# Building the S4 convolution kernel's power tables from scaled activations in blocks of 224 channels, in place of argument matmuls in blocks of 48

## The chip, the cores and the metric

The kernel runs on one core of a Trainium2 chip. The metric is the device time of one execution in microseconds (us): the median of 5 runs is 1173.82 us (1171.51 to 1175.57). The engines are TensorE (PE in the profile, its weight loads PEld), the vector engine (DVE), the scalar engine (ACT), GpSimd (POOL) and SyncE (SP), which issues DMAs.

## The reference

Two layers run on separate inputs, and their outputs are joined along the last axis. A is a linear attention with softmax feature maps (16 heads of 28, sequence 2048, width 448). B, which matters here, is a diagonal state-space convolution: for each of 448 channels d there are N = 256 complex modes n, and

```
dt    = exp(log_dt)[:, None]
logdA = dt * (A_re + 1j * A_im)                       # 448 x 256
dB    = dt * (B_re + 1j * B_im)
P     = exp(logdA[:, :, None] * l[None, None, :])     # l = 0 .. 2047 (as bf16)
K     = einsum("dn,dnl,dn->dl", Cc, P, dB).real       # the convolution kernel
y     = irfft(rfft(pad(u)) * rfft(pad(K)))[:L] + u * Dskip
```

## The kernel before, in words

The program has three stretches. `hedgehog_attention` computes A. `ssm_coefficients` and `ssm_build_K` build K. `ssm_fft_conv` makes the sine and cosine constants of the Fourier steps and does the convolution in several passes through DRAM. Each stretch needs the memory or the results of the one before it, so they follow each other with little overlap. The instructions are written in program order; the Tile framework orders them on each engine's queue and adds the semaphore waits. Each queue runs in order.

K is built by splitting l = 64 h + l' with h = 0..31 and l' = 0..64. With w = exp(dt(A_re + i A_im)), the 128 modes of one chunk on the partitions (`nch` = 0, 1), U[h] = C dB w^(64h) and W[l'] = w^l', K is the real part of the sum over modes of U[h] W[l']. That is one pair of matmuls for each channel and chunk: `kps` += UR^T WR and UI^T WI, each 128 modes deep, 32 columns of weights (h) and 65 moving columns (l'). Four channels, one from each quarter g of the 448, use the four 32-column groups of the array (`tile_position=(0, 32*g)`), so four such matmuls run side by side. UI carries the minus sign.

Before the change `ssm_coefficients` makes dt A twice: on 4 x 112 channel rows, split into two bf16 parts and written to DRAM as `coefd` (lines 457 to 484), and once more in the layout modes x channels (`A_nd`, `TH_nd`, `CBR_nd`, `CBIN_nd`), from 12 transposing DMAs (line 504). `ssm_build_K` then loops over 2 chunks and 10 super-blocks `sb` of 12 x 4 = 48 channels (the last has 16):

- U is built by doubling on the vector engine (lines 650 to 655): k = 1, 2, 4, 8, 16, six bf16 operations each, on k x 48 elements; the powers w^(64k) (`P`, lines 566 to 587) are copied to dense 48-wide tiles by GpSimd first (lines 637, 638).
- W is built through PSUM: `coefblk` is loaded from `coefd`, and TensorE multiplies it by the ramp `Rconst` (lines 665, 667) to give the arguments l' dt A of 18 channels at a time in `args`, which has one buffer. ACT takes Exp of one half and twice Sin of the other (lines 684, 685, 687; Exp and Sin need different activation tables), and the vector engine multiplies (lines 693, 695).
- `emit_kmm` (lines 604, 606) does the pairs of matmuls of the super-block before. The sums of the first chunk are copied to `Ts` by ACT (line 611), those of the second added by the vector engine (line 613).

At the end `Ts` goes to DRAM as `kd` (line 705), and the Fourier part starts; its first vector operation that is long is `n1f` (line 759).

Of the kernel before, what the change touches and what calls it, by code (L numbers as in the profile page):

```python
# [451 lines left out]
def ssm_coefficients(tc, B_A_re, B_A_im, B_B_re, B_B_im, B_C_re, B_C_im, B_log_dt, coefd, base_pool):  # L452
    nc = tc.nc
    with tc.tile_pool(name="coef_in", bufs=1) as inp_pool, \
         tc.tile_pool(name="coef_w", bufs=1, side="right") as w:
        for dc in range(4):
            d0 = 112 * dc
            rows = 112
            tiles = {}
            for nm, src in (("Are", B_A_re), ("Aim", B_A_im)):  # L460
                t = inp_pool.tile([112, SSM_N], BF16, name=f"ci_{nm}", tag=nm)
                nc.sync.dma_start(out=t[:, :], in_=src[d0:d0 + rows, :])
                tiles[nm] = t
            ldt = inp_pool.tile([112, 1], BF16, name="ci_ldt", tag="ldt")
            nc.sync.dma_start(out=ldt[:, :], in_=B_log_dt[d0:d0 + rows].unsqueeze(1))
            dt32 = w.tile([112, 1], F32, name="dt32", tag="dt32")
            nc.scalar.activation(dt32[:, :], ldt[:, :], ACT.Exp)
            dtb = w.tile([112, 1], BF16, name="dtb", tag="dtb")
            nc.vector.tensor_copy(dtb[:, :], dt32[:, :])
            dt = w.tile([112, 1], F32, name="dt", tag="dt")  # L470
            nc.vector.tensor_copy(dt[:, :], dtb[:, :])
            a = w.tile([112, SSM_N], F32, name="a", tag="a")
            nc.vector.tensor_scalar_mul(a[:, :], tiles["Are"][:, :], dt[:, :])
            th = w.tile([112, SSM_N], F32, name="th", tag="th")
            nc.vector.tensor_scalar_mul(th[:, :], tiles["Aim"][:, :], dt[:, :])
            for ti, src_t in enumerate((a, th)):
                b1 = w.tile([112, SSM_N], BF16, name="b1", tag="b1")
                nc.vector.tensor_copy(b1[:, :], src_t[:, :])
                dif = w.tile([112, SSM_N], F32, name="dcf", tag="dcf")
                nc.vector.tensor_tensor(out=dif[:, :], in0=src_t[:, :], in1=b1[:, :], op=ALU.subtract)  # L480
                b2 = w.tile([112, SSM_N], BF16, name="b2", tag="b2")
                nc.vector.tensor_copy(b2[:, :], dif[:, :])
# [41 lines left out]
def build_R(tc, pool):  # L524
    nc = tc.nc
    with tc.tile_pool(name="rtmp", bufs=1) as tp:
        pidx = tp.tile([4, 1], I32, name="pidx")
# [16 lines left out]
    return R


def ssm_build_K(tc, coefd, kd, A_nd, TH_nd, CBR_nd, CBIN_nd, base_pool, dbg=False):
# [4 lines left out]
    with tc.tile_pool(name="k_const", bufs=1) as cpool, \
         tc.tile_pool(name="k_ts", bufs=1) as tspool, \
         tc.tile_pool(name="k_coef", bufs=2) as coefpool, \
         tc.tile_pool(name="k_hi", bufs=2) as hipool, \
         tc.tile_pool(name="k_tab", bufs=2) as tabpool, \
         tc.tile_pool(name="k_psarg", bufs=1, space=bass.MemoryType.PSUM) as psa_pool, \
         tc.tile_pool(name="k_psk", bufs=1, space=bass.MemoryType.PSUM) as psk_pool:
# [4 lines left out]
        for nch in range(2):
            P = {}
            amp1 = base_pool.tile([128, D_MODEL], F32, name="amp1", tag="amp1")
            nc.scalar.activation(amp1[:, :], A_nd[:, nch, :], ACT.Exp, scale=64.0)
            c1 = base_pool.tile([128, D_MODEL], F32, name="c1", tag="c1")
            nc.scalar.activation(c1[:, :], TH_nd[:, nch, :], ACT.Sin, bias=bias_hp[:, :], scale=64.0)
            s1 = base_pool.tile([128, D_MODEL], F32, name="s1", tag="s1")
            nc.scalar.activation(s1[:, :], TH_nd[:, nch, :], ACT.Sin, scale=-64.0)  # L570
            pr = base_pool.tile([128, D_MODEL], BF16, name="p1r", tag="p1r")
            pim = base_pool.tile([128, D_MODEL], BF16, name="p1i", tag="p1i")
            nc.vector.tensor_tensor(out=pr[:, :], in0=amp1[:, :], in1=c1[:, :], op=ALU.mult)
            nc.vector.tensor_tensor(out=pim[:, :], in0=amp1[:, :], in1=s1[:, :], op=ALU.mult)
            P[1] = (pr, pim)
# [12 lines left out]
            pending = []  # L588

            def emit_kmm(item):  # L590
                sbp, nqp, URp, UIp, WRp, WIp, nchp = item
                half = (nqp + 1) // 2
                stripes = [(0, half)]
                if nqp > half:
                    stripes.append((half, nqp))
                for si_, (q0, q1) in enumerate(stripes):
                    nqs = q1 - q0
                    kps = psk_pool.tile([128, 512], F32, name="kps", tag=f"kps{si_}")
                    for dql in range(q0, q1):
                        cs = dql - q0  # L600
                        for g in range(4):
                            slot = 4 * dql + g
                            outap = kps[32 * g:32 * (g + 1), cs * N_LO:(cs + 1) * N_LO]
                            nc.tensor.matmul(outap, lhsT=URp[:, :, slot], rhs=WRp[:, slot, :],  # L604
                                             start=True, stop=False, tile_position=(0, 32 * g))
                            nc.tensor.matmul(outap, lhsT=UIp[:, :, slot], rhs=WIp[:, slot, :],  # L606
                                             start=False, stop=True, tile_position=(0, 32 * g))
                    dq0 = sbp + q0
                    in_view = kps[:, 0:nqs * N_LO].rearrange("p (c l) -> p l c", c=nqs)
                    if nchp == 0:  # L610
                        nc.scalar.copy(Ts[:, :, dq0:dq0 + nqs], in_view)
                    else:
                        nc.vector.tensor_tensor(out=Ts[:, :, dq0:dq0 + nqs],
                                                in0=Ts[:, :, dq0:dq0 + nqs], in1=in_view, op=ALU.add)
# [469 lines left out]
```

## Time and profile before

| | us |
|---|---|
| median of 5 runs | 1173.82 |
| the profiled execution | 1177.62 |
| its span, first to last instruction | 1175.8 |
| busy in it: DVE, PE, ACT, POOL | 591.9, 539.4, 463.6, 101.6 |
| attention, start to 308.3 | 308.3 |
| coefficients and transposes, to 362.7 | 54.4 |
| the loop that builds K, to 773.5 | 410.8 |
| `kd` write and Fourier part, to the end | 402.3 |

The profile is of one execution. No engine is busy for more than half of the span, so shares over the whole span say little here; the stages have to be read one at a time.

### The profile page before, as it was taken

The numbers are of one execution on the slowest core, as the hardware profiler recorded it, in microseconds if no ns is written. First come the engines' busy times: TensorE is split into PE (matmuls) and PEld (weight loads), VectorE is DVE, ScalarE is ACT, GpSimd is POOL, SyncE is SP. The second block draws the span as 40 slices with busy tenths as digits, with TensorE's granted clock in tenths as the row PEclk, the third lists the DMA queues.
The fourth block names the chain that finished last, engine by engine and source line by source line (L and its number), as shares of the span: only waits on it lengthen the run. The fifth ranks groups of instructions, "written<-read, shape, count | busy, mean of one in ns | idle before, by whom it ended". The sixth has DMA issues, their size and how long they took to land.

```text
span 1175.8 us, 13968 instructions
## 1 busy us (share of the span) xinstructions
PE 539.4 (46%) x5285; PEld 251.0 (21%) x5291; DVE 591.9 (50%) x1288; ACT 463.6 (39%) x488; POOL 101.6 (9%) x260
## 2 busy tenths in 40 slices
PE   1986543846802433334334444402433444263298
PEld 0221100511201333333233333300111111010021
DVE  1339337526639765594756767429322224832500
ACT  0113320001216778878688788724212222031000
POOL 1000010000004221131211110010000000010000
PEclk9995655667965555555555555555555555555555
DMA  5000000000230000000000000050675666057511
GB/s 127 1 0 1 0 0 0 4 7 0 81 71 10 4 3 4 4 3 3 3 4 3 3 5 3 3 95 0 170 220 167 149 150 238 16 140 186 221 31 31
DMA packets 68011, 63.63 MB, mean 54 GB/s; under 512 B 33704, under 2 KB 64608, under 8 KB 67712
## 3 DMA queue, kind: packets, MB, share of 16 engines
q1 hardware_dynamic: 34554, 32.59, 10.3%
q10 hardware_dynamic: 31758, 23.73, 7.6%
q0 software_dynamic: 1632, 6.42, 1.6%
q8 instruction: 41, 0.67, 0.2%
q14 instruction: 26, 0.21, 0.1%
HBM read 30.73 MB, written 28.52 MB: 50 GB/s over the span
## 4 chain that ended last, share of the span: by engine, by line
DVE 33%; PE 29%; DMA 19%; ACT 9%; issue 7%; ACTq 1%; SPq 0%; POOL 0%; DVEq 0%; POOLq 0%
PE args L665 3%; DVE WR L693 3%; PE args L667 3%; PE ps_qk L195 3%; ACT L685 3%; PE ops L1013 2%; ACT CL L685 2%; PE ops L1011 2%; DVE UR L652 2%; DVE rt L650 2%; DVE rt L653 2%; DVE UI L655 2%; DMA xin<-kd 2%; PE num_ps L396 2%; DMA s2k<-SD_u 2%
## 5 line engine op out<-in xcount | busy, mean ns | idle before, releaser
L604 PE MATMUL kps<-WR,UR 128*32 128x65 bf16 x896 | 53.5, 257 | 203.3 <-DVE WR L693 198.2
L665 PE MATMUL args<-Rconst,coefblk 4*128 4x65 bf16 x896 | 105.1, 239 | 77.9 <-ACT SL L687 43.0
L665 PEld LDWEIGHTS <-coefblk 4*128 4x128 bf16 x896 | 96.7, 126 | 151.0 <-issue 145.4
L667 PEld LDWEIGHTS <-coefblk 4*128 4x128 bf16 x896 | 98.5, 128 | 42.5 <-issue 42.5
L667 PE MATMUL args<-Rconst,coefblk 4*128 4x65 bf16 x896 | 105.8, 240 | 0.0
L875 PE MATMUL psA<-xin,FA 32*128 32x448 bf16 x128 | 51.8, 565 | 97.7 <-DVE stgA L888 34.5
L684 ACT ACTIVATE E<-args 128x1170 bf16<-128x1170 f32 (+3 forms) x58 | 58.5, 1008 | 68.9 <-PE args L667 68.9
L693 DVE TENSOR_TENSOR WR<-E,CL 128x1170 bf16<-128x1170 bf16 (+3 forms) x58 | 39.6, 682 | 71.0 <-ACT CL L685 71.0
L685 ACT ACT_TABLE_LOAD x58 | 74.4, 1283 | 1.0
L684 ACT ACT_TABLE_LOAD x57 | 73.1, 1283 | 3.9 <-DVE WI L695 2.4
L888 DVE CAST stgA<-psA 128x1792 bf16<-128x1792 f32 x16 | 32.4, 2022 | 70.2 <-PE psA L875 43.2
L685 ACT ACTIVATE CL<-args,bias_hp 128x1170 bf16<-128x1170 f32 (+3 forms) x58 | 63.7, 1099 | 0.7
L412 ACT CAST rbc_sb<-rbc_ps 128x512 bf16<-128x512 f32 (+1 forms) x16 | 9.3, 585 | 133.7 <-PE rbc_ps L405 133.3
L687 ACT ACTIVATE SL<-args 128x1170 bf16<-128x1170 f32 (+3 forms) x58 | 58.0, 1000 | 0.0
L886 ACT CAST stgA<-psA 128x1792 bf16<-128x1792 f32 x16 | 26.4, 1652 | 79.1 <-PE psA L875 45.1
L604 PEld LDWEIGHTS <-UR 128*32 128x32 bf16 x896 | 37.0, 159 | 80.6 <-issue 62.3
L1011 PE MATMUL ops<-ZA,IA 128*32 128x448 bf16 x64 | 35.4, 556 | 34.5 <-DMA ZA<-ZD 34.5
L195 PE MATMUL ps_qk<-xT,Wqkv 128*128 128x512 bf16 (+3 forms) x125 | 37.3, 405 | 29.3 <-DMA xT<-in_A_x_dram 26.0
L909 PE MATMUL xps<-s2k,CB 128*32 128x448 bf16 x256 | 27.4, 534 | 47.2 <-DMA s2k<-SD_u 23.3
L606 PE MATMUL kps<-WI,UI 128*32 128x65 bf16 x896 | 43.9, 255 | 6.4 <-DVE WI L695 5.1
L875 PEld LDWEIGHTS <-FA 32*128 32x128 bf16 x128 | 17.0, 134 | 131.9 <-issue 103.9
L606 PEld LDWEIGHTS <-UI 128*32 128x32 bf16 x896 | 37.3, 163 | 31.1 <-issue 25.8
(265 smaller groups left out, 1152.2 us busy)
## 6 DMA issues: line engine op xcount, KB each, us to landing
ZA<-ZD SPq DMA_DIRECT2D x1, 7168.0 KB
SD_u<-stgA SPq DMA_DIRECT2D x8, 448.0 KB
SD_u<-stgA ACTq DMA_DIRECT2D x8, 448.0 KB
SD_k<-stgA SPq DMA_DIRECT2D x8, 448.0 KB
SD_k<-stgA ACTq DMA_DIRECT2D x8, 448.0 KB
s2k<-SD_u ACTq DMA_DIRECT2D x3, 896.0 KB
s2k<-SD_u SPq DMA_DIRECT2D x3, 896.0 KB
s2k<-SD_k ACTq DMA_DIRECT2D x3, 896.0 KB
```

Source lines behind the costliest of these rows:

```text
L195: nc.tensor.matmul(ps[plo:phi, sc * 512:(sc + 1) * 512], lhsT=Wt[dci][dplo:dphi, fcol0:fcol0 + frows], rhs=xT[dci][dplo:dphi, sc * 512:(sc ...
L604: nc.tensor.matmul(outap, lhsT=URp[:, :, slot], rhs=WRp[:, slot, :], start=True, stop=False, tile_position=(0, 32 * g))
L606: nc.tensor.matmul(outap, lhsT=UIp[:, :, slot], rhs=WIp[:, slot, :], start=False, stop=True, tile_position=(0, 32 * g))
L665: nc.tensor.matmul(args[:, j * 512 + si * N_LO:j * 512 + (si + 1) * N_LO], lhsT=coef[0:4, slot, :], rhs=R[0:4, 0, :], start=True, stop=True)
L667: nc.tensor.matmul(args[:, j * 512 + (3 + si) * N_LO:j * 512 + (4 + si) * N_LO], lhsT=coef[0:4, slot, :], rhs=R[0:4, 1, :], start=True, st ...
L684: nc.scalar.activation(E[:, b0:b0 + nb, 0:ns * N_LO], argview(0), ACT.Exp)
L685: nc.scalar.activation(CL[:, b0:b0 + nb, 0:ns * N_LO], argview(3 * N_LO), ACT.Sin, bias=bias_hp[:, :])
L687: nc.scalar.activation(SL[:, b0:b0 + nb, 0:ns * N_LO], argview(3 * N_LO), ACT.Sin)
L693: nc.vector.tensor_tensor(out=wr_v, in0=E[:, b0:b0 + nb, 0:ns * N_LO], in1=CL[:, b0:b0 + nb, 0:ns * N_LO], op=ALU.mult)
L875: nc.tensor.matmul(ps[:, n2l * 512:n2l * 512 + D_MODEL], lhsT=FA2[0:32, :], rhs=xt[0:32, 4 * j + n2l, :], start=True, stop=True,)
L888: nc.vector.tensor_copy(stg[:, jr:jr + 4, :], in_view)
L1011: nc.tensor.matmul(ops[32 * g2:32 * (g2 + 1), 0:D_MODEL], lhsT=IA[:, :], rhs=ZA[:, m2, :], start=True, stop=False, tile_position=(0, 32 * g2))
```

## The change

`coefd`, `build_R` and everything that read them go: the 4 x 112 rows of coefficients, their DMAs, `coefblk`, the argument matmuls, the GpSimd copies. W is computed straight from `A_nd` and `TH_nd`: for each l' one ACT instruction with `scale=l'` on 224 channels. The channel block grows from 48 to 224 (`h` = 0, 1; 56 from each quarter), so that there are four blocks in all (2 chunks x 2 halves), B0 to B3 below. Only l' = 0..48 come from ACT; l' = 49..64 are w^32 W[l'-32], one complex product on the vector engine (`_cmul`), and w^32 is `Q32`. `E` holds all 48 exponentials of a block, the sines come in 8 chunks of 6 l' in two buffers each. W is now laid out with l' outside and channels inside, so a matmul's moving operand `WR[:, :, slot]` has a step of 224 elements (448 bytes) where it was contiguous, and the weights `UR[:, :, slot]` have a step of 224 elements where it was 48. `WR` and `WI` have one buffer for all blocks, `UR` and `UI` two, `kps` two.

```diff
-def ssm_coefficients(tc, ..., B_log_dt, coefd, base_pool):
+def ssm_coefficients(tc, ..., B_log_dt, base_pool):
-        for dc in range(4):
...
-                nc.sync.dma_start(out=coefd[2 * ti, d0:d0 + rows, :], in_=b1[:, :])
-                nc.scalar.dma_start(out=coefd[2 * ti + 1, d0:d0 + rows, :], in_=b2[:, :])
...
+def _cmul(nc, out_r, out_i, ar, ai, brb, bib, t1, t2, sub):
+    nc.vector.tensor_tensor(out=t1, in0=ar, in1=brb, op=ALU.mult)
+    nc.vector.tensor_tensor(out=t2, in0=ai, in1=bib, op=ALU.mult)
+    nc.vector.tensor_tensor(out=out_r, in0=t1, in1=t2, op=ALU.subtract)
+    nc.vector.tensor_tensor(out=t1, in0=ar, in1=bib, op=ALU.mult)
+    nc.vector.tensor_tensor(out=t2, in0=ai, in1=brb, op=ALU.mult)
+    nc.vector.tensor_tensor(out=out_i, in0=t1, in1=t2, op=ALU.add)
...
-            for sb in range(0, NDQ, SBQ):
+            for h in range(2):
+                q_off = HQ * h
+                def dv(t2d):
+                    return t2d.rearrange("p (g q) -> p g q", g=4)[:, :, q_off:q_off + HQ]
...
                 for k in (1, 2, 4, 8, 16):
                     pr, pim = P[k]
-                    nc.gpsimd.tensor_copy(cr[:, 0:nds]..., dview(pr[:, :]))
-                    nc.gpsimd.tensor_copy(ci_[:, 0:nds]..., dview(pim[:, :]))
+                    prb = dv(pr[:, :]).unsqueeze(1).to_broadcast([128, k, 4, HQ])
+                    pib = dv(pim[:, :]).unsqueeze(1).to_broadcast([128, k, 4, HQ])
+                    _cmul(nc, gq(UR[:, k:2 * k, :]), gq(UI[:, k:2 * k, :]), gq(UR[:, 0:k, :]), gq(UI[:, 0:k, :]),
+                          prb, pib, gq(t1[:, 0:k, :]), gq(t2[:, 0:k, :]), False)
...
-                        nc.tensor.matmul(args[...], lhsT=coef[0:4, slot, :], rhs=R[0:4, 0, :], start=True, stop=True)
-                        nc.tensor.matmul(args[...], lhsT=coef[0:4, slot, :], rhs=R[0:4, 1, :], start=True, stop=True)
...
-                        nc.scalar.activation(E[:, b0:b0 + nb, 0:ns * N_LO], argview(0), ACT.Exp)
+                for l in range(1, LA):
+                    nc.scalar.activation(E[:, l - 1, :]..., dv(A_nd[:, nch, :]), ACT.Exp, scale=float(l))
+                for l0 in range(1, LA, CH):
+                    C = tabpool.tile([128, CH, NS], BF16, name="CL", tag="CL")
+                    S = tabpool.tile([128, CH, NS], BF16, name="SL", tag="SL")
+                    for l in range(l0, l0 + CH):
+                        nc.scalar.activation(C[:, l - l0, :]..., dv(TH_nd[:, nch, :]), ACT.Sin, bias=bias_hp[:, :], scale=float(l))
+                        nc.scalar.activation(S[:, l - l0, :]..., dv(TH_nd[:, nch, :]), ACT.Sin, scale=float(l))
+                    nc.vector.tensor_tensor(out=WR[:, l0:l0 + CH, :], in0=E[:, l0 - 1:l0 - 1 + CH, :], in1=C[:, :, :], op=ALU.mult)
+                    nc.vector.tensor_tensor(out=WI[:, l0:l0 + CH, :], in0=E[:, l0 - 1:l0 - 1 + CH, :], in1=S[:, :, :], op=ALU.mult)
+                nt = N_LO - LA
+                _cmul(nc, gq(WR[:, LA:N_LO, :]), gq(WI[:, LA:N_LO, :]), gq(WR[:, LA - 32:N_LO - 32, :]),
+                      gq(WI[:, LA - 32:N_LO - 32, :]), qrb, qib, gq(t1[:, 0:nt, :]), gq(t2[:, 0:nt, :]), False)
...
-                            nc.tensor.matmul(outap, lhsT=URp[:, :, slot], rhs=WRp[:, slot, :],
+                            nc.tensor.matmul(outap, lhsT=UR[:, :, slot], rhs=WR[:, :, slot],
                                              start=True, stop=False, tile_position=(0, 32 * g))
```

How the queues stand now is shown at three places. The first is ACT's queue in the loop. Before, each group of up to 18 channels has two table loads, an Exp that waits for TensorE, and two Sin:

```order
L684 ACT_TABLE_LOAD [waits DVE_49]
L684 ACTIVATE E<-args 128x1170 [waits PE_49]
L685 ACT_TABLE_LOAD
L685 ACTIVATE CL<-args,bias_hp 128x1170 [waits Activation_49]
L687 ACTIVATE SL<-args 128x1170 [waits Activation_49]
```

Now, at the passage from block B0 to B1 (line 572 is Exp, 578 and 580 are Sin, 604 is the copy of `kps`, with the line numbers of the changed kernel):

```order
L580 ACTIVATE SL<-TH_nd 128x224
L572 ACT_TABLE_LOAD
L572 ACTIVATE E<-A_nd 128x224 [waits DVE_49]
L572 ACTIVATE E<-A_nd 128x224 x22
L604 CAST Ts<-kps 128x65x7 [waits PE_49]
L572 ACTIVATE E<-A_nd 128x224 x4
L604 CAST Ts<-kps 128x65x7 [waits PE_49]
```

The 48 Exp of B1 stand together behind one table load, with the eight copies of B0's sums between them; the sines of B1 follow behind all of these.

The second place is the vector engine's queue where a block begins. Before, the first steps of the doubling are on 48 elements and the products wait for ACT alone:

```order
L650 TENSOR_TENSOR rt_4534<-UR,pc8r 128x384 [waits DVE_49]
L651 TENSOR_TENSOR rt_4535<-UI,pc8i 128x384
L652 TENSOR_TENSOR UR<-rt_4534,rt_4535 128x384 [waits DVE_49]
L693 TENSOR_TENSOR WR<-E,CL 128x1170 [waits Activation_49]
L653 TENSOR_TENSOR rt_4534<-UR,pc8i 128x384 [waits DVE_49]
```

Now, in B1 (494 to 499 are `_cmul`, 582 and 584 the products):

```order
L498 TENSOR_TENSOR rt_2858<-UI,p8r 128x1792
L582 TENSOR_TENSOR WR<-E,CL 128x1344 [waits PE_49,Activation_49]
L499 TENSOR_TENSOR UI<-rt_2857,rt_2858 128x1792 [waits DVE_49]
L584 TENSOR_TENSOR WI<-E,SL 128x1344 [waits PE_49,Activation_49]
L494 TENSOR_TENSOR rt_2857<-UR,p16r 128x3584 [waits DVE_49]
L495 TENSOR_TENSOR rt_2858<-UI,p16i 128x3584
L582 TENSOR_TENSOR WR<-E,CL 128x1344 [waits Activation_49]
L496 TENSOR_TENSOR UR<-rt_2857,rt_2858 128x3584 [waits DVE_49]
```

The long steps of the doubling now stand between the products of the first chunks, and the first product of a block waits for TensorE too, since `WR` has one buffer.

The third place is the end of a block on the same queue, in B0:

```order
L494 TENSOR_TENSOR rt_2174<-WR,p1rl 128x3584 [waits DVE_49]
L495 TENSOR_TENSOR rt_2175<-WI,p1il 128x3584 [waits DVE_49]
L582 TENSOR_TENSOR WR<-E,CL 128x1344 [waits Activation_49]
L584 TENSOR_TENSOR WI<-E,SL 128x1344 [waits Activation_49]
L496 TENSOR_TENSOR WR<-rt_2174,rt_2175 128x3584 [waits DVE_49]
L582 TENSOR_TENSOR WR<-E,CL 128x1344 [waits Activation_49]
L584 TENSOR_TENSOR WI<-E,SL 128x1344 [waits Activation_49]
L497 TENSOR_TENSOR rt_2174<-WR,p1il 128x3584 [waits DVE_49]
L498 TENSOR_TENSOR rt_2175<-WI,p1rl 128x3584
L499 TENSOR_TENSOR WI<-rt_2174,rt_2175 128x3584 [waits DVE_49]
```

The product for l' = 49..64 is begun after chunk 5, and its last three operations stand behind the products of chunk 7; the matmuls of the block wait for the last of them.

## Rows read from the trace of the kernel before

**Rows 1.** Busy time by stage (windows view; after each sum, the instruction count).

```profile
core 0: us, PE busy (x) PEld busy (x) DVE busy (x) ACT busy (x) POOL busy (x), PEclk, DMA share, GB/s
0.00:308.30 308.30, 190.84 (x1006) 59.58 (x1012) 140.91 (x221) 50.08 (x63) 8.40 (x27) 0.73 0.06 14
308.30:362.70 54.40, 15.26 (x89) 6.67 (x89) 31.75 (x91) 10.39 (x19) 2.06 (x6) 0.69 0.32 83
362.70:773.50 410.80, 157.46 (x3548) 140.08 (x3547) 268.61 (x811) 330.17 (x311) 73.44 (x197) 0.50 0.02 4
773.50:1175.80 402.30, 175.79 (x643) 44.69 (x643) 150.63 (x168) 72.96 (x97) 17.67 (x30) 0.51 0.47 132
```

**Rows 2.** Waits in the loop, longest first (us in total, times, longest).

```profile
PE kps L604 <- DVE WR L693: 198.2, 54, 9.6
DVE WR L693 <- ACT CL L685: 71.0, 27, 5.4
ACT E L684 <- PE args L667: 68.9, 53, 5.5
```

**Rows 3.** Chain that ended last (start us, us, what): around the loop.

```profile
328.85 1.22 ACTq L504
...
354.53 2.47 DMA tin_Cre<-in_B_C_re_dram
...
360.21 0.68 ACT c L568
...
773.54 15.27 DMA kd<-Ts
...
789.49 4.10 DVE n1f L759
```

**Rows 4.** ACT, 305 to 790 us, by form (count, busy us, mean ns, idle before).

```profile
L685 ACT ACT_TABLE_LOAD x58 | 74.4, 1283 | 1.0
L684 ACT ACT_TABLE_LOAD x57 | 73.1, 1283 | 3.9 <-DVE WI L695 2.4 <-DVE UI L655 0.5
...
L684 ACT ACTIVATE E<-args 128x1170 bf16<-128x1170 f32 x36 | 41.3, 1146 | 52.2 <-PE args L667 52.2
...
L684 ACT ACTIVATE E<-args 128x780 bf16<-128x780 f32 x18 | 14.8, 821 | 15.6 <-PE args L667 15.6
...
L611 ACT CAST Ts<-kps 128x390 bf16<-128x390 f32 x18 | 9.2, 511 | 1.9 <-PE kps L606 1.9
...
L568 ACT ACTIVATE c<-TH_nd,bias_hp 128x448 f32<-128x448 f32 x2 | 1.3, 668 | 3.3 <-DVE bias_hp L561 3.3
...
L566 ACT ACTIVATE amp<-A_nd 128x448 f32<-128x448 f32 x2 | 1.2, 576 | 10.4 <-DVE ttmp L516 10.4
```

**Rows 5.** Timeline: two activations of ACT back to back (start us, us).

```profile
486.42 1.24 ACT L685 ACTIVATE CL<-args,bias_hp 128x1170 bf16<-128x1170 f32 x1
487.56 1.14 ACT L687 ACTIVATE SL<-args 128x1170 bf16<-128x1170 f32 x1
```

**Rows 6.** DVE, 305 to 790 us, by form.

```profile
L613 DVE TENSOR_TENSOR Ts<-Ts,kps 128x390 bf16<-128x390 bf16 x18 | 10.0, 558 | 15.0 <-PE kps L606 15.0
...
L650 DVE TENSOR_TENSOR rt<-UR,pc16r 128x768 bf16<-128x768 bf16 x18 | 10.0, 557 | 1.5
...
L650 DVE TENSOR_TENSOR rt<-UR,pc8r 128x384 bf16<-128x384 bf16 x18 | 6.4, 358 | 1.4
...
L573 DVE TENSOR_TENSOR p1r<-amp,c 128x448 bf16<-128x448 f32 x2 | 1.2, 620 | 0.7 <-ACT c L568 0.7
```

**Rows 7.** Timeline of PE inside `emit_kmm` (start us, us; x4: four merged).

```profile
484.14 0.32 PE L604 MATMUL kps<-WR,UR 128*32 128x65 bf16 x4
...
484.20 0.32 PE L606 MATMUL kps<-WI,UI 128*32 128x65 bf16 x4
...
484.27 0.32 PE L604 MATMUL kps<-WR,UR 128*32 128x65 bf16 x4
```

**Rows 8.** Weight loads: 128 contiguous columns, and 32 columns with a step.

```profile
L665 PEld LDWEIGHTS <-coefblk 4*128 4x128 bf16 x896 | 96.7, 126 | 151.0 <-issue 145.4 <-DMA coefblk<-coefd 3.2 <-PE args L667 0.4
...
L604 PEld LDWEIGHTS <-UR 128*32 128x32 bf16 x896 | 37.0, 159 | 80.6 <-issue 62.3 <-DVE WR L693 9.9 <-DVE UR L652 7.4
```

More of the change, by code (lines that the diff above doesn't have):

```diff
@@ L449, with ssm_coefficients @@
 N_ARG = 2 * N_LO
-def ssm_coefficients(tc, B_A_re, B_A_im, B_B_re, B_B_im, B_C_re, B_C_im, B_log_dt, coefd, base_pool):
+def ssm_coefficients(tc, B_A_re, B_A_im, B_B_re, B_B_im, B_C_re, B_C_im, B_log_dt, base_pool):
     nc = tc.nc
-    with tc.tile_pool(name="coef_in", bufs=1) as inp_pool, \
-         tc.tile_pool(name="coef_w", bufs=1, side="right") as w:
-        for dc in range(4):
[L457 to L482, printed above, removed]
-                nc.sync.dma_start(out=coefd[2 * ti, d0:d0 + rows, :], in_=b1[:, :])
-                nc.scalar.dma_start(out=coefd[2 * ti + 1, d0:d0 + rows, :], in_=b2[:, :])
     A_nd = base_pool.tile([128, 2, D_MODEL], F32, name="A_nd")
@@ L562, in ssm_build_K, with make_pow @@
         Ts = tspool.tile([128, N_LO, NDQ], BF16, name="Ts")
+        WR = wpool.tile([128, N_LO, NS], BF16, name="WR")
+        WI = wpool.tile([128, N_LO, NS], BF16, name="WI")
+        nc.gpsimd.memset(WR[:, 0, :], 1.0)
+        nc.gpsimd.memset(WI[:, 0, :], 0.0)
         for nch in range(2):
[L564 to L575, printed above, removed]
+            def make_pow(scale, tagp, neg_sin):
+                amp = base_pool.tile([128, D_MODEL], F32, name="amp", tag="amp")
+                nc.scalar.activation(amp[:, :], A_nd[:, nch, :], ACT.Exp, scale=float(scale))
+                cv = base_pool.tile([128, D_MODEL], F32, name="cv", tag="cv")
+                nc.scalar.activation(cv[:, :], TH_nd[:, nch, :], ACT.Sin, bias=bias_hp[:, :], scale=float(scale))
+                sv = base_pool.tile([128, D_MODEL], F32, name="sv", tag="sv")
+                nc.scalar.activation(sv[:, :], TH_nd[:, nch, :], ACT.Sin,
+                                     scale=float(-scale if neg_sin else scale))
+                pr = base_pool.tile([128, D_MODEL], BF16, name=f"p1r{tagp}", tag=f"p1r{tagp}")
+                pi = base_pool.tile([128, D_MODEL], BF16, name=f"p1i{tagp}", tag=f"p1i{tagp}")
+                nc.vector.tensor_tensor(out=pr[:, :], in0=amp[:, :], in1=cv[:, :], op=ALU.mult)
+                nc.vector.tensor_tensor(out=pi[:, :], in0=amp[:, :], in1=sv[:, :], op=ALU.mult)
+                return pr, pi
+            P = {1: make_pow(64.0, "h", True)}
+            Q32 = make_pow(32.0, "l", False)
             for k in (2, 4, 8, 16):
@@ L587, in ssm_build_K @@
                 P[k] = (nr, ni)
[L588 to L603, printed above, removed]
-                            nc.tensor.matmul(outap, lhsT=URp[:, :, slot], rhs=WRp[:, slot, :],
[L605 to L614, printed above, removed]
@@ new lines, in ssm_build_K @@
+                nt = N_LO - LA
+                qrb = dv(Q32[0][:, :]).unsqueeze(1).to_broadcast([128, nt, 4, HQ])
+                qib = dv(Q32[1][:, :]).unsqueeze(1).to_broadcast([128, nt, 4, HQ])
+                _cmul(nc, gq(WR[:, LA:N_LO, :]), gq(WI[:, LA:N_LO, :]), gq(WR[:, LA - 32:N_LO - 32, :]),
+                      gq(WI[:, LA - 32:N_LO - 32, :]), qrb, qib, gq(t1[:, 0:nt, :]), gq(t2[:, 0:nt, :]), False)
+                for q0 in range(0, HQ, 7):
+                    kps = psk_pool.tile([128, 512], F32, name="kps", tag="kps")
+                    for cs in range(7):
+                        for g in range(4):
+                            slot = HQ * g + q0 + cs
+                            outap = kps[32 * g:32 * (g + 1), cs * N_LO:(cs + 1) * N_LO]
+                            nc.tensor.matmul(outap, lhsT=UR[:, :, slot], rhs=WR[:, :, slot],
+                                             start=True, stop=False, tile_position=(0, 32 * g))
+                            nc.tensor.matmul(outap, lhsT=UI[:, :, slot], rhs=WI[:, :, slot],
+                                             start=False, stop=True, tile_position=(0, 32 * g))
+                    dq0 = q_off + q0
+                    in_view = kps[:, 0:7 * N_LO].rearrange("p (c l) -> p l c", c=7)
+                    if nch == 0:
+                        nc.scalar.copy(Ts[:, :, dq0:dq0 + 7], in_view)
+                    else:
+                        nc.vector.tensor_tensor(out=Ts[:, :, dq0:dq0 + 7],
+                                                in0=Ts[:, :, dq0:dq0 + 7], in1=in_view, op=ALU.add)
```

144 lines of the change are left out of this document (29 added, 115 removed).

## The prediction

> **What bounds the kernel now.** I read the busy time by stage first [rows 1]. The loop that builds K takes 410.8 us, and the stages before and after it (308.3 + 54.4, and 402.3) hold almost nothing that the change touches. In the loop ACT is busy 330.2 us, DVE 268.6, PE 157.5. Then the waits [rows 2]: PE stands 198.2 us before its K matmuls for DVE's product, DVE 71.0 us for ACT's sine, ACT 68.9 us for PE's arguments. So it is a ring through one `args` buffer, in which ACT works longest. Then what ACT does [rows 4]: of its 330 us, 74.4 + 73.1 = 147.5 us are 115 table loads of 1283 ns, more than Exp or either Sin costs. Last, the chain of waits for the ends of the loop [rows 3]: the transposes run from 328.85 to 354.53 + 2.47 = 357.0, the first cosine starts at 360.21, `kd` is sent at 773.54, lands 15.27 later, and the Fourier part's vector work starts at 789.49.
>
> The profiled execution took 1177.62 us, 1.8 above its span; the median of the runs, 1173.82, is 3.8 below it. I sum against the profiled execution and take off the 3.8 at the end.
>
> **Prices.** DVE, bf16: 557 ns for 768 elements and 358 for 384 [rows 6], so 0.518 ns per element and 0.16 us fixed: 224 elements 0.275 us, 448 0.39, 896 0.62, 1344 0.86, 1792 1.09, 3584 2.02. With f32 operands, 448 elements cost 0.62. ACT: Exp on 1170 and 780 elements takes 1146 and 821 ns, 0.833 ns per element [rows 4]. From the 448-element forms that read SBUF (576 ns, with a bias tile 668) 224 elements less make 389 and 482 ns. A sine that follows another starts 0.10 us before its end (486.42 + 1.24 against 487.56) [rows 5]; so I charge 0.29 for Exp, 0.29 + 0.38 = 0.67 for a Cos/Sin pair, 4.0 for a chunk of 6, 13.9 for 48 Exp. If the 0.10 is not won between short ones, a chunk is 5.2 and the Exp 18.7. A copy of `kps` (455 elements) is 0.57 on ACT (511 for 390) and 0.63 on DVE (558 for 390). PE: four real matmuls start each 0.13 us, four imaginary ones between (484.14, 484.20, 484.27) [rows 7], so 8 in 0.13 us and 448 per block in 7.3 us.
>
> One price the trace lacks: a moving operand with a step. Below, it can cost nothing (7.3 us a block). Above, the nearest row is the weight load with a step, 159 ns for 32 columns against 126 for 128 contiguous ones [rows 8]: 5.0 ns a column, so 65 columns take 323 ns, a group's two matmuls 0.65, 56 rounds 36.4 us. I take twice the contiguous price, 14.6 us, nearer the low end, because the weights had a step already and four such loads hide within each 0.065 us of the pace above; I keep both ends. The Trainium skill ("Advanced Engine Details and Errata", section Memory Cachelines) says that SBUF is read in 16-byte lines and an access that changes line each time pays. It speaks against this layout, where each of the 65 columns is on its own line; it gives no figure, and by it the sum moves from the low end toward the upper one. No row here shows it for a moving operand.
>
> **Part by part.** *Removed.* The coefficient rows cost the path only where they delay the transposes behind the last output copies: I credit 3 us of the gap before 328.85 (bounds 0 and 8). The GpSimd copies (73 us busy) and the loads of `coefblk` lay beside other work: 0. The argument matmuls, and with them ACT's 68.9 us of waits, go. *Start.* The 12 transposes stay, so they end at 354.0. The bias tile still comes after them, the first cosine about 5.5 later. Then DVE stands between it and the first product of B0: 22 operations on 448 elements in f32 for the powers and w^32, at 0.62 or a little less, 12.9 us, and the doubling to k = 4 with two operations of k = 8, 9.6 (five at 0.275, six at 0.39, six at 0.62, two at 1.09): 22.5 us. First product: 382. ACT needs 19 us for the same stretch and waits.
>
> *A block* has on DVE: doubling 6 x (0.275 + 0.39 + 0.62 + 1.09 + 2.02) = 26.4, products 16 x 0.86 = 13.8, the l' >= 49 product 6 x 2.02 = 12.1, and 14 us of powers per mode chunk. On ACT: 13.9 + 8 x 4.0 and table loads. I walk the queues from each block's first product (t = 0).
>
> B0: DVE does 8 products, 4 steps of k = 8 and 6 of k = 16 interleaved: 6.9 + 4.4 + 12.1 = 23.4. ACT's chunk 5 needs the buffer freed there: done 27.4, chunk 6 at 32.0, chunk 7 at 36.6 (with the next chunk's cosine and sine). Last product 38.6, last three operations of the tail 44.7. ACT then does load 1.3, Exp 13.9, eight copies 4.6, load 1.3, chunk 4.0: 63.7. DVE from 44.7: doubling to k = 4, 7.7, ten operations of powers 6.6, five of k = 8 5.5: 64.5. PE's 7.3 or 14.6 us lie beside this. B0 takes 64.5.
>
> B1: products of chunks 0 to 2 with the long steps, 5.2 + 1.1 + 12.1 = 18.4; chunk 4 done 22.4; then the next chunk's amplitude with two loads, 3.2, chunk 5 at 29.4, 6 at 34.6, 7 at 38.6; last product 40.6, tail 47.3. ACT to the next chunk 0: 40.6 + 25.1 = 65.7; DVE 47.3 + 18 = 65.3. B1 takes 65.8.
>
> B2: no amplitude, so last product 37.4, tail 43.5. ACT 37.4 + 1.3 + 13.9 + 1.3 + 4.0 = 57.9; DVE 43.5 + 7.7 + 2.2 + eight adds 5.0 = 58.4. B2 takes 58.4.
>
> B3: as B0 to 44.7, then the matmuls 7.3 and the last add: 52.7.
>
> Sum 241.4; PE at 14.6 adds 1.7 (copies later on ACT), 3.0, 0 and 7.3, so 12. `kd` is sent at 382 + 241.4 + 12 = 635.5 in place of 773.5: 138 us earlier. What follows has its instructions and waits unchanged: 402.3. 1177.6 - 138 = 1039.6, less 3.8: **1036 us**.
>
> Bounds: PE at 7.3 and 5 us less at the start give 1019. Without the 0.10 us overlap the four blocks grow by 8.5, 10.6, 9 and 2.1 by the same walk: 1066. The Trainium skill ("VectorE: DVE Perf Modes", section on the TRN2 errata) says that VectorE and ScalarE pay a fixed latency for each instruction with an SBUF source and advises tiles of 512 or more; 576 instructions on 224 elements go against it. The row agrees that about 0.2 of the 0.39 us is fixed, and the rule's time is this 1066.
>
> **The rivals.**
> 1. *The strided matmuls decide.* At the upper price, 36.4 us a block, ACT's copies and then `WR`'s single buffer hold the next block: B0 passes at 44.7 + 36.4 + 6.9 = 88.0 in place of 64.5, B1 at 90.6 in place of 65.8, B2 at 79.9 in place of 58.4, B3 29.1 later: 99 us over the sum at 7.3 (1024): 1123. For it: [rows 8]. Against it: the pace of [rows 7] with stepped weights. 13%.
> 2. *DVE loses its rate.* The doubling and the tail now read a third operand in pieces of 56 out of 448, repeated. If this went at about 1.04 ns per element, the rate of the add that reads PSUM (558 ns for 390), 41,664 + 21,504 elements a block cost 33 us more, on the engine that is nearly always late: +120 of 132: 1156. Against it: today's repeated operand, in pieces of 48, runs at 0.518. 8%. This is also how the change could do little.
> 3. *Slower: the four column groups stop overlapping.* If their stepped reads wait for one another, the 448 matmuls of a block stand one behind another at up to 323 ns: 145 us a block. Above 15 us a block all four blocks pay; the sum is 1024 + 4k - 47 for k us a block, level with before at k = 49, 0.11 us per matmul, seven times today's 16 ns. At 323 ns it is 1557, at half that 1268. For it: the upper price is 20 times today's pace if nothing overlaps. Against it: stepped weight loads overlap now. 5%.
>
> **How the numbers follow.** The walk with its bounds (1019 to 1066) has 70%, rival 1 13%, rival 2 8%, rival 3 5%; 4% are left for a walk that is too slow on handovers nobody waits on, under 1010. The range 1010 to 1125 leaves out rivals 2 and 3, that edge and part of rival 1. A measurement tells 0.2% (2.3 us): faster 0.94, within 0.01, slower 0.05.
>
> **What the profile of the changed kernel would show.** ACT in the loop at about 17 table loads and 576 short activations of 0.39 and 0.48 us that start 0.29 and 0.38 apart. DVE busy some 250 us of a loop of about 255, doubling steps of 2.0 us at 3584 elements (3.9 would be rival 2). The K matmuls in four bursts of 7 to 15 us, with ACT's copies behind them; bursts of 36 us and a wait of DVE's first product for PE are rival 1, matmuls without overlap rival 3. GpSimd empty. `kd` near 636. The forecast is wrong if the gap between blocks is set by PE, or if the start of the loop moves by more than 8 us.

## The result, and the profile after

The changed kernel takes 1000.24 us (median of 8 runs, 998.98 to 1003.29) against 1174.27 (15 runs): ratio 0.852, 95% interval 0.850 to 0.853. That is 36 us less than forecast and 10 us below the low end of the range. The direction and the place of the gain were right, the size was not.

The profiled execution took 999.33 us (span 997.5). Busy time by stage, columns as in [rows 1]:

```profile
core 0: us, PE busy (x) PEld busy (x) DVE busy (x) ACT busy (x) POOL busy (x), PEclk, DMA share, GB/s
0.00:307.80 307.80, 190.62 (x1000) 58.91 (x1006) 139.69 (x219) 49.35 (x62) 8.39 (x27) 0.74 0.06 13
307.80:358.50 50.70, 14.89 (x59) 5.22 (x58) 19.38 (x38) 16.17 (x34) 0.51 (x2) 0.69 0.25 66
358.50:600.30 241.80, 53.95 (x1792) 52.49 (x1792) 227.63 (x278) 207.48 (x596) 0.13 (x1) 0.59 0.01 3
600.30:997.50 397.20, 174.11 (x643) 43.85 (x643) 150.39 (x168) 72.84 (x97) 17.61 (x30) 0.52 0.47 133
```

The loop takes 241.8 us in place of 410.8, and now DVE (227.6 us busy) and ACT (207.5) nearly fill it. The chain of waits shows the same marks as [rows 3]; the forecast had `kd` sent at 635.5:

```profile
351.00 2.29 DMA tin_Cre<-in_B_C_re_dram
...
600.33 15.02 DMA kd<-Ts
615.85 4.05 DVE n1f L664
```

From `kd` to the end it is 397.2 us, 5.1 less than before. So the profiled run is 40.3 us under the forecast's 1039.6 for a profiled execution: 35.2 of it up to `kd`, 5.1 behind it.

ACT from 358 to 601 us by form (answers to [rows 4]: count, busy us, mean ns, idle before):

```profile
L578 ACT ACTIVATE CL<-TH_nd,bias_hp 128x224 bf16<-128x224 f32 x192 | 86.7, 468 | 8.0 <-DVE WR L582 8.0
L580 ACT ACTIVATE SL<-TH_nd 128x224 bf16<-128x224 f32 x192 | 68.8, 374 | 2.5 <-DVE WI L584 2.3
L572 ACT ACTIVATE E<-A_nd 128x224 bf16<-128x224 f32 x174 | 50.8, 379 | 0.1
L604 ACT CAST Ts<-kps 128x455 bf16<-128x455 f32 x16 | 10.3, 642 | 0.8 <-PE kps L599 0.4
L572 ACT ACT_TABLE_LOAD x5 | 6.4, 1283 | 0.1
L578 ACT ACT_TABLE_LOAD x5 | 6.4, 1283 | 0.0
```

Forecast were 0.48, 0.39, 0.39 and 0.57 us: the prices from [rows 4] held but for the copies, which took 0.64 (1.1 us more for all 16), and 115 table loads became 14 in this stretch. DVE by form (370 to 620 us, answers to [rows 6]):

```profile
L582 DVE TENSOR_TENSOR WR<-E,CL 128x1344 bf16<-128x1344 bf16 x32 | 27.2, 850 | 2.4 <-ACT CL L578 2.4
L606 DVE TENSOR_TENSOR Ts<-Ts,kps 128x455 bf16<-128x455 bf16 x16 | 10.7, 667 | 9.2 <-PE kps L599 9.2
...
L494 DVE TENSOR_TENSOR rt<-UR,p16r 128x3584 bf16<-128x3584 bf16 x4 | 8.1, 2016 | 0.0
```

Forecast were 0.86, 0.63 and 2.02: again the prices held (the adds took 0.67), and rival 2 (3.9 us for the longest) is out. But a duration is not what an instruction costs its queue. DVE's timeline (start us, us) at the end of B0:

```profile
410.28 0.85 DVE L582 TENSOR_TENSOR WR<-E,CL 128x1344 bf16<-128x1344 bf16 x1
411.05 0.85 DVE L584 TENSOR_TENSOR WI<-E,SL 128x1344 bf16<-128x1344 bf16 x1
411.82 2.02 DVE L497 TENSOR_TENSOR rt<-WR,p1il 128x3584 bf16<-128x3584 bf16 x1
413.75 2.02 DVE L498 TENSOR_TENSOR rt<-WI,p1rl 128x3584 bf16<-128x3584 bf16 x1
415.80 2.03 DVE L499 TENSOR_TENSOR WI<-rt,rt 128x3584 bf16<-128x3584 bf16 x1
```

A product of 0.85 is followed after 0.77, an operation of 2.02 after 1.93: DVE starts the next 0.08 us before the end. One that needs the result just made waits it out (L499 reads what L498 wrote: 2.05), and so does one that writes over a tile just read (an L496 of 0.28 us from 418.36, and the L497 behind it, which refills its operand, starts at 418.67). The trace of the kernel before shows the same, a little ahead of the place of [rows 5] (DVE's timeline):

```profile
480.81 0.76 DVE L693 TENSOR_TENSOR WR<-E,CL 128x1170 bf16<-128x1170 bf16 x1
481.49 0.37 DVE L654 TENSOR_TENSOR rt<-UI,pc8r 128x384 bf16<-128x384 bf16 x1
```

Here 0.76 is followed after 0.68.

PE in the last block (timeline; answers to [rows 7]):

```profile
585.83 0.38 PE L597 MATMUL kps<-WR,UR 128*32 128x65 bf16 x4
585.96 0.36 PE L599 MATMUL kps<-WI,UI 128*32 128x65 bf16 x4
586.08 0.36 PE L597 MATMUL kps<-WR,UR 128*32 128x65 bf16 x4
...
586.30 0.37 PE L597 MATMUL kps<-WR,UR 128*32 128x65 bf16 x4
```

Eight matmuls take 0.23 us here, 0.13 before: 13 us a block.

### The profile page after: what moved, and what is told of

Its sections match the earlier page's. It is cut to its first block, busy times and chain, and to the rows that moved or that the text cites. A ratio compares the mean times of both kernels' runs of the same rounds, so it can differ in the third digit from the quotient of the medians.

```text
span 997.5 us, 9371 instructions
## 1 busy us (share of the span) xinstructions
PE 433.6 (43%) x3493; PEld 160.5 (16%) x3499; DVE 537.1 (54%) x701; ACT 345.9 (35%) x788; POOL 26.6 (3%) x60
## 4 chain that ended last, share of the span: by engine, by line
DVE 34%; PE 31%; DMA 22%; ACT 8%; issue 4%; ACTq 1%; SPq 0%; DVEq 0%; POOLq 0%
PE ps_qk L195 4%; PE ops L918 3%; PE ops L916 3%; PE kps L599 3%; PE kps L597 2%; DMA xin<-kd 2%; PE num_ps L396 2%; DMA s2k<-SD_u 2%; DVE WI L584 2%; DVE WR L582 2%; PE psA L780 2%; PE ps_pq L268 2%; DMA SD_u<-stgA 2%; DVE rt L498 2%; DVE rt L497 2%
## 5 line engine op out<-in xcount | busy, mean ns | idle before, releaser
L578 ACT ACTIVATE CL<-TH_nd,bias_hp 128x224 bf16<-128x224 f32 x192 | 86.7, 468 | 8.0 <-DVE WR L582 8.0
L597 PEld LDWEIGHTS <-UR 128*32 128x32 bf16 x896 | 46.6, 136 | 215.4 <-issue 154.0
L580 ACT ACTIVATE SL<-TH_nd 128x224 bf16<-128x224 f32 x192 | 68.8, 374 | 2.5 <-DVE WI L584 2.3
L572 ACT ACTIVATE E<-A_nd 128x224 bf16<-128x224 f32 x192 | 56.0, 378 | 0.1
L599 PEld LDWEIGHTS <-UI 128*32 128x32 bf16 x896 | 46.2, 135 | 6.5 <-DVE WI L499 6.5
L881 PE MATMUL zps<-YF,IB 32*128 32x448 bf16 x64 | 22.9, 530 | 41.8 <-DVE YF L868 24.4
L893 DVE CAST Zs<-zps 128x448 bf16<-128x448 f32 x32 | 20.0, 625 | 33.6 <-PE zps L884 32.1
L780 PEld LDWEIGHTS <-FA 32*128 32x128 bf16 x128 | 16.7, 133 | 131.5 <-issue 78.8
L891 ACT CAST Zs<-zps 128x448 bf16<-128x448 f32 x32 | 17.0, 532 | 60.0 <-PE zps L884 30.1
L918 PE MATMUL ops<-UD,IDT 32*32 32x448 bf16 x64 | 34.7, 551 | 1.4 <-DVE UD L908 1.4
L231 PE MATMUL ps_pk<-WBD,kT 128*128 128x448 bf16 x64 | 27.0, 540 | 14.0 <-ACT ek L240 12.0
```

What stands on the lines that cost most here:

```text
L231: nc.tensor.matmul(ps[:, 0:D_MODEL], lhsT=kT[dci][dplo:dphi, tt * 128:(tt + 1) * 128], rhs=WBD[dci][dplo:dphi, 0:D_MODEL], start=(dj == 0) ...
L572: nc.scalar.activation(E[:, l - 1, :].rearrange("p (g q) -> p g q", g=4), dv(A_nd[:, nch, :]), ACT.Exp, scale=float(l))
L578: nc.scalar.activation(C[:, l - l0, :].rearrange("p (g q) -> p g q", g=4), dv(TH_nd[:, nch, :]), ACT.Sin, bias=bias_hp[:, :], scale=float(l))
L580: nc.scalar.activation(S[:, l - l0, :].rearrange("p (g q) -> p g q", g=4), dv(TH_nd[:, nch, :]), ACT.Sin, scale=float(l))
L597: nc.tensor.matmul(outap, lhsT=UR[:, :, slot], rhs=WR[:, :, slot], start=True, stop=False, tile_position=(0, 32 * g))
L599: nc.tensor.matmul(outap, lhsT=UI[:, :, slot], rhs=WI[:, :, slot], start=False, stop=True, tile_position=(0, 32 * g))
```

## The experiments

Theory A: two queues, ACT and DVE, bound the loop together, each charged from the start of an instruction to the start of the next. To put numbers on it I walked both queues in the order in which the program has them, from the first product on, with the measured starts. The tail is the complex product for l' = 49..64 that ends a block. The walk of the changed kernel meets the measured ends of the four tails (417.8, 475.6, 531.3, 585.8) within 0.8 us and `kd` within 1.5; its prices come from the same trace, so its test is what it says of the edits. The loop's start moves from run to run (first product at 374.4 to 379.7 us where the start was not edited), so I also give the stretch from the first product to the end of the last add, 221.5 us in the changed kernel. It is read from one profiled execution of each kernel; the ratio is to the kernel before. e3 to e7 don't compute K: e3 and e4 read other elements than the ones needed, e5 to e7 leave work out.

| kernel | us (median) | ratio, 95% | first product to last add |
|---|---|---|---|
| changed kernel | 1000.2 | 0.850 to 0.853 | 221.5 |
| e1_split | 1013.8 | 0.862 to 0.866 | 238.2 |
| e2_one_tile | 1008.3 | 0.857 to 0.862 | 229.0 |
| e3_rhs_row | 994.1 | 0.845 to 0.850 | 215.9 |
| e4_lhs_row | 999.4 | 0.848 to 0.854 | 220.1 |
| e5_less_dve | 998.8 | 0.847 to 0.852 | 220.7 |
| e6_less_act | 1002.4 | 0.851 to 0.855 | 218.4 |
| e7_less_both | 997.1 | 0.847 to 0.850 | 214.1 |
| v1_pool_hoist | 1015.6 | 0.862 to 0.867 | 235.7 |
| v2_split_last | 1006.0 | 0.854 to 0.860 | 227.5 |
| e8_hoist_only | 1001.9 | 0.851 to 0.854 | 222.8 |
| e9_exp_chunk | 1050.8 | one run | 274.5 |
| e10_half_block | 1071.0 | one run | 301.5 |

**e1: what an operation on DVE costs.**

```
-  _cmul(... UR[:, k:2*k] ...)                       # k = 16; the tail likewise
+  for j in range(0, 16, 4):
+      _cmul(... UR[:, 16+j:20+j], ... prb[:, j:j+4] ...)
```

> Each of the 12 longest vector operations of a block (3584 elements) is cut in four of 896: 144 instructions more on DVE, no element more. Theory A (DVE starts an instruction 0.08 us before the one before it ends, so a cut costs 4 x 0.535 - 1.935 = 0.2 us per operation): 48 x 0.2 = 9.7 us on DVE; a walk of ACT's and DVE's queues in program order, charged from start to start, gives +9 us at kd: 1009. Theory B (every instruction costs its whole duration, as the prediction charged, and the gain over the prediction comes from elsewhere): 48 x (4 x 0.617 - 2.016) = 21.7 us, by the walk +24: 1024. Theory C (DVE is not what sets the loop): within 3 us of 1000.

Measured +13.5 us, +16.7 in the stretch. The pieces, on DVE's timeline:

```profile
389.01 0.62 DVE L497 TENSOR_TENSOR rt<-UR,p16i 128x896 bf16<-128x896 bf16 x1
389.55 0.62 DVE L498 TENSOR_TENSOR rt<-UI,p16r 128x896 bf16<-128x896 bf16 x1
390.08 0.62 DVE L495 TENSOR_TENSOR rt<-UI,p16i 128x896 bf16<-128x896 bf16 x1
```

0.62 long, 0.535 apart. Counted from start to start and without its waits, DVE's work from the first product to the last add grows from 209.0 to 218.9 us: 9.9, where A's price gives 9.7 and B's 21.7. So a cut costs what A says. The other 6.8 us of the stretch are waits, 5.1 of them for ACT's cosines (7.5 for 2.4); the scheduler set the pieces elsewhere among the products, and the walk, +9, did not have that. `kd` comes 16.2 us later, as far from A's 9 as from B's 24, so the total does not tell the two apart: the price does. C's 0 is out.

**e2: who waits for a freed buffer.**

```
-  C = tabpool.tile([128, CH, NS], ...);  S = tabpool.tile([128, CH, NS], ...)
+  CS = tabpool.tile([128, 2, CH, NS], ...);  C, S = CS[:, 0], CS[:, 1]
```

> Cosine and sine of a chunk share one tile, so that ACT's next chunk waits until both products have read it, as the prediction's walk assumed; same work. Theory A (in the real order the cosines refill their buffer while the sine product still waits; the prediction's walk lost its 5 us a block there): the walk of the queues in program order gives +9 us at kd, 1009, with the last product of a block later against its first by some 3 us. Theory B (the handover of these buffers is free, all of the gain over the prediction is DVE's overlap of 0.08 us): 1000, within 2 us.

Measured +8.1 us, +7.5 in the stretch: A. In the changed kernel (ACT's timeline) chunk 5's cosines start behind the cosine product alone, and fill the time until the sine product is done:

```profile
397.27 2.34 ACT L578 ACTIVATE CL<-TH_nd,bias_hp 128x224 bf16<-128x224 f32 x6 [0.29 <-DVE WR L582]
399.52 0.56 ACT L529 ACTIVATE sv<-TH_nd 128x448 f32<-128x448 f32 x1
399.99 1.78 ACT L580 ACTIVATE SL<-TH_nd 128x224 bf16<-128x224 f32 x6
```

With one tile, the waits (total, times, longest):

```profile
ACT CS L578 <- DVE WI L584: 17.6, 8, 3.3
DVE WR L582 <- ACT CS L578: 9.6, 6, 2.3
```

Against 10.3 and 2.4 us in the changed kernel: the two queues hand the wait back and forth.

**e3 and e4: which operand of the K matmuls costs.**

```
e3:  rhs=WR[:, :, slot]   ->  rhs=WR[:, slot % 65, 65*(slot % 3):65*(slot % 3) + 65]
e4:  lhsT=UR[:, :, slot]  ->  lhsT=UR[:, slot % 32, 32*(slot % 7):32*(slot % 7) + 32]
```

(and the imaginary parts likewise.)

> The K matmuls read 65 contiguous elements of WR and WI in place of 65 elements a row apart (wrong values of K; same instructions). If the step of the moving operand is what makes 8 matmuls take 0.228 us: 0.13 us again, 7.3 us a block in place of 13; three of the four blocks hide it, the last shows it: kd 6 to 8 us earlier, 993. If the weights' step, or the accumulation, makes it: bursts of 13 us and 1000. If the clock makes it (0.5 to 1.0 in the last burst): bursts of 13 us in the first part and less in the second, 1000.

> The K matmuls take their weights from 32 contiguous elements of UR and UI in place of 32 a row apart (wrong values of K; same instructions). If the moving operand's step makes the 0.228 us per 8 matmuls: unchanged, 13 us a block, 1000 within 2 us. If the weights' step makes it: 7.3 us a block, 993.

e3: -6.2 us, -5.6 in the stretch. PE's timeline in its last block:

```profile
584.34 0.30 PE L597 MATMUL kps<-WR,UR 128*32 128x65 bf16 x4
584.39 0.30 PE L599 MATMUL kps<-WI,UI 128*32 128x65 bf16 x4
584.45 0.30 PE L597 MATMUL kps<-WR,UR 128*32 128x65 bf16 x4
```

Eight in 0.115 us. e4, with contiguous weights and the moving operand's step kept:

```profile
588.07 0.31 PE L597 MATMUL kps<-WR,UR 128*32 128x65 bf16 x4
588.18 0.31 PE L599 MATMUL kps<-WI,UI 128*32 128x65 bf16 x4
588.29 0.31 PE L597 MATMUL kps<-WR,UR 128*32 128x65 bf16 x4
```

Eight in 0.22: unchanged, and so is its time (the interval holds the changed kernel's ratio). So the moving operand's step is the price. The clock is not, as the changed kernel's last burst shows (PE busy, granted clock):

```profile
585.80:590.00 4.20, 4.18 (x147) 0.50 0.01 4
590.00:598.00 8.00, 8.00 (x290) 1.00 0.01 4
```

35 matmuls per us at 1.2 GHz, 36 at 2.4. Of e3's 5.6 us, 3.2 lie behind the last tail (10.6 us to the last add, 13.8 in the changed kernel) and 2.4 ahead of it, so the first three blocks hide most of their matmuls, but perhaps not all: in e4, with the same burst, the last tail is 1.0 us nearer too.

**e5, e6, e7: which queue bounds the loop.**

```
e5:  if nch == 1: P[k] = P0[k]; continue             # in the loop over k = 2, 4, 8, 16
e6:  - nc.scalar.copy(Ts[:, :, dq0:dq0 + 7], in_view)
     + nc.gpsimd.memset(Ts[:, :, :], 0.0)            # once, ahead of the loop
e7:  both
```

> The 20 operations that square the powers of w for the second mode chunk are left out and the first chunk's powers used (wrong values): 20 x 0.53 = 10.7 us less on DVE. Measured from the first product to the last add, 221.5 us before this edit. Theory A (ACT and DVE bound the loop together, each nearly without a wait): the walk of the two queues gives -2: 998. Theory B (DVE alone sets it): -10.7: 989. Theory C (ACT alone): 0: 1000.

> ACT's 16 copies out of kps for the first mode chunk are left out and Ts starts as zeros (wrong values: that chunk's part of K is missing): 16 x 0.6 = 9.6 us less on ACT. From the first product to the last add, 221.5 before: theory A (bound together): the walk gives -2.5: 998. Theory B (DVE alone): 0: 1000. Theory C (ACT alone): -9.6: 990.

> Both edits at once (the squares of the second chunk and the 16 copies left out, wrong values). Theory A: more than the sum of the two alone, the walk gives -7.3 (alone -2 and -2.5): 993. Theory B (DVE alone): -10.7, the same as without the squares only: 989. Theory C (ACT alone): -9.6, the same as without the copies only: 990.

Measured in the stretch: -0.7, -3.1 and -7.4 us (e4, whose vector and scalar queues are the changed kernel's, differs from it by 1.3, so differences of that size tell nothing), where A had -2, -2.5 and -7.3; B had -10.7, 0 and -10.7, C 0, -9.6 and -9.6. The waits of e5 and of e6 show the handing over:

```profile
DVE WR L586 <- ACT CL L582: 9.7, 4, 2.8
```

```profile
ACT CL L579 <- DVE WR L583: 13.0, 7, 2.9
ACT SL L581 <- DVE WI L585: 3.3, 7, 1.2
```

In e5 DVE's work is 8.1 us shorter from start to start, and 7.3 come back as more waiting for ACT (9.7 for 2.4). In e6, of 9.6 us less on ACT, 6 come back as more waiting for DVE (16.3 for 10.3). The totals of e6 and e7 hide this, since their start is later (first product at 383.7 and 381.4): GpSimd's new memset holds DVE up, here in e6:

```profile
358.20 5.41 DVE L561 CAST UR<-CBR_nd 128x224 bf16<-128x224 f32 x1
```

```profile
357.32 6.17 POOL L520 MEMSET Ts<- 128x7280 bf16 x1 [32.03 <-DVE ttmp L485]
```

A cast that takes 0.27 us in the changed kernel took 5.41 and ended 0.1 us behind the memset.

**v1 and e8: both queues shorter, with the whole computation.**

```
e8:  + amps[(n, sc)]: the four Exp of A_nd * 64 and * 32, taken ahead of the loop over nch
v1:  e8, and  peng = nc.gpsimd if nch == 1 else nc.vector   # for the powers of w
```

> A version with the whole computation: the second chunk's powers of w are worked out on GpSimd, which is idle (24 vector operations, 12.8 us off DVE), and the four amplitudes are taken beside the first Exp, which saves 4 table loads of 1.28 us. Theory A: both queues get shorter, the walk gives -5.7: 994.5, if GpSimd's operations don't slow DVE and are done before DVE needs them (18 us of slack for each of the two stages). Theory B (DVE alone): -12.8: 987. Theory C (ACT alone): -5.1: 995. If GpSimd and DVE hold each other up, by more than 6 us in all: 1000 or above.

> The four amplitudes beside the first Exp (4 table loads of 1.28 us less on ACT) without the work on GpSimd. Theory A: ACT's 5 us less are of no use where DVE is as late: the walk gives 0: 1000. If the 15 us that the GpSimd version lost came from taking the amplitudes early: 1015. If ACT alone sets the loop: 995.

e8: no gain (222.8 against 221.5), so the amplitudes' table loads were not on the path. v1: +15 us, the last expectation. The loss is made where GpSimd works: the tail of B1 ends as in the changed kernel (97.3 us after the first product, 97.5 there), that of B2 14.0 us later. DVE crawls there (DVE, then GpSimd, in v1):

```profile
475.17 1.23 DVE L495 TENSOR_TENSOR rt<-UI,p1ih 128x224 bf16<-128x224 bf16 x1
476.44 0.98 DVE L496 TENSOR_TENSOR UR<-rt,rt 128x224 bf16<-128x224 bf16 x1
477.45 1.21 DVE L497 TENSOR_TENSOR rt<-UR,p1ih 128x224 bf16<-128x224 bf16 x1
```

```profile
475.08 1.20 POOL L539 TENSOR_TENSOR p1rl<-amp,cv 128x448 bf16<-128x448 f32 x1
476.35 0.93 POOL L550 TENSOR_TENSOR sq<-p1rh 128x448 f32<-128x448 bf16 x1
```

0.27 us became 1.0 to 1.2, and the first two end 0.1 us after the GpSimd instruction beside them, as if the two engines took turns, one instruction each.

**v2: the last block's matmuls ahead of the tail.**

```
+  for (la, lb) in ((0, 49), (49, 65)):              # last block only, 8 banks
+      ... rhs=WR[:, la:lb, slot] ... kps[..., cs*65 + la:cs*65 + lb]
```

> The whole computation. In the last block the K matmuls of the 49 rows that are ready before the tail are issued first, into eight banks of PSUM, and those of the other 16 rows after it. Theory A (only the last block's matmuls lie open, 13 us at 8 per 0.228 us, and the step of the moving operand sets them, so 16 columns take 16/65 of it, at least 3.2 us and at most the 7.3 us of contiguous rows): kd 6 to 9 us earlier, 992. If the number of matmuls sets the pace: 13 us after the tail as before, 1000.

Measured +5.8 us, +6.0 in the stretch. The first row of PE's timeline and the waits say why:

```profile
577.43 0.79 PE L602 MATMUL kps<-WR,UR 128*32 128x49 bf16 x7 [34.68 <-DVE WR L582]
```

```profile
PE kps L604 <- issue: 6.5, 4, 1.9
```

The 49 rows are complete only at the last product, 6.7 us before the tail ends, and 896 short matmuls from there take until 603, with 6.5 us in which nothing that the profile shows held PE; what did stays open. The expectation had put their start before the tail and their price by columns; both were wrong.

**e9 and e10: the choices inside the change.** e9 moves the `E` activation into the loop over l of its chunk; e10 sets `HQ = 28` and four `h`.

> Exp of six rows stands with the cosines and sines of the same six rows, in place of all 48 ahead: some 50 table loads more of 1.28 us in the loop (62 in place of 10 from the first product on); same work. Theory A: ACT then sets the loop alone, the walk gives +56: 1056. If DVE alone sets the loop: about 1000.

> Blocks of 112 channels in place of 224: twice as many instructions on half the elements, 576 more on ACT and some 220 more on DVE; same work. Theory A (each has a part that doesn't depend on the elements, 0.10 us from start to start on ACT and 0.08 on DVE): ACT +83 us, the walk gives +75 to 80: 1078. If the time goes with the elements alone: 1000.

1050.8 and 1071.0 us, +53 and +80 in the stretch, where the walk had +56 and +75 to 80. The totals, forecast as 1056 and 1078, came out 5 and 7 lower: the first products of these two runs came 3.6 and 5.4 us earlier than the changed kernel's. In e9 ACT is busy 255.2 of 257.4 us up to the last tail; in e10 a cosine on half the elements costs 376 ns in place of 468:

```profile
L578 ACT ACTIVATE CL<-TH_nd,bias_hp 128x112 bf16<-128x112 f32 x334 | 124.2, 376 | 0.5 <-DVE WR L582 0.4
```

No version with the whole computation is faster than the changed kernel; e3's 6 us would need another layout of `WR`.

## Why the prediction was right or wrong

*Right.* What bounds the kernel, what goes (ACT's waits for the arguments, the table loads), the prices of ACT and DVE as durations (but for 0.07 us on a copy and 0.04 on an add), the start of the stage (transposes end at 353.3, forecast 354.0), and the stage behind `kd` to 5 us. Rivals 1 and 3 fell: a block's matmuls take 13 us, not 36 or 145, and DVE's first products don't wait for PE. Rival 2 fell with the 2.02 us above. Neither of the prediction's signs of being wrong showed: PE does not set the gap between blocks, and the first product came at 378.1, 3.9 us early, where 8 was the limit.

*Wrong: the size of the four blocks and of their start.* From the forecast's 635.5 (its terms as printed add up to 635.4) to the measured 600.3 for `kd`, in the order in which the walk takes the steps back (in another order the sizes would differ; where a run has a step of its own, its number stands beside it):

- *Durations summed on DVE: -14.2 us.* The prediction charged each vector operation its full duration ("products 16 x 0.86 = 13.8"), while ACT was given its 0.10 us of overlap from [rows 5]. Of 290 vector operations between 353 and 601 us, 244 start before the end of the one before, 20 us in all. Of the 14.2, 3.2 lie before the first product (24.8 us from the transposes, forecast 28) and 11, by the walk, after it. e1 shows the price. The Trainium skill ("Perfetto Trace Analysis", section DVE / Act Engine Instruction) says that the reported end is the write's acknowledgement, while the next instruction may begin to read once the one before has left the ALUs; the 0.08 us agrees, and it stood in the trace of before. I had looked for it on one engine only.
- *"ACT's chunk 5 needs the buffer freed there": -8.9 us.* The walk let a chunk wait for both products. In the program's order the cosines go ahead as soon as their own buffer is free, and with that the walk's 38.6 us from the first to the end of the last product of B0 becomes 36.1 (33.8 with DVE's overlap, as measured: 378.1 to 411.9). e2 restores the assumption and costs 7.5.
- *Two things put on the path that lie beside it: -8.9 us.* 3.2 for the amplitude in B1, which ACT did while DVE was late anyway (e8: taking it out gives nothing); and 1.7 + 3.0 for PE's slower matmuls, since ACT's copies stand among the Exp and not behind them. The other 1.0 is what is left of the hand walk. This part is worked out by the walk; only the amplitude has a run of its own. The prediction left 4% for a time under 1010 by handovers nobody waits on; this step and the one before it, 17.8 us of the 35.2, are largely such.
- *PE at 14.6 us a block: -3.9 us.* It took 13: the middle that was taken was good, and most of it is open in the last block only, as forecast. From the end of the last tail to `kd` it is 14.6 us where the forecast had 15.3, so 0.7 of the 3.9 is seen there; the rest is the walk's, in the blocks before, and no run shows it. The Trainium skill ("Advanced Engine Details and Errata", section Memory Cachelines) is borne out as far as it goes: the step costs 0.228 us for 0.13, and e3 takes it away. That it would speak against the change is not: three blocks of four hide most of it, and the kernel is 174 us faster.
- Transposes -0.7; the rest, +1.4, is what the walk misses of the measured end.

*Not settled.* The 5.1 us behind `kd`. Its instructions are the same; in e1 to e4 this stage takes 396.3 to 399.7 us against 402.3. One profile of the kernel before doesn't tell how much of this is the run's own scatter.

The range failed with the sum: its low end kept everything at full duration and took only the start and PE from below. The bound that was missing was the same overlap on DVE, 14 us, which alone would have put the low end near 1005 (1019 - 14), still above the measured 1000: the buffers were missing from it too.

## What to carry to other kernels

Before summing a queue, read two neighbours on its timeline and charge start to start, on every engine of the sum; 244 overlaps of 0.08 us are 20 us of work here and, by the walk, 14 of the time. Walk the queues in the program's real order, one buffer at a time, and put a term on the path only where the other queue would not have been late anyway. Where two queues are both full, relief on one of them comes back as a wait: test by relieving each alone and both.
